# A lower rank for batch 0's evacuations in the planned opening of an attention and mixing kernel

## The chip, the core and the metric

The kernel runs on one core of a Trainium2 chip. The metric is the device time of one execution in microseconds, lower is better. The core has TensorE (PE in the rows; its weight loads are PEld), VectorE (DVE), ScalarE (ACT), GpSimd (POOL) and SyncE (SP), on whose queue the kernel starts its transfers.

## The reference

There are 8 batches, 8 heads, 576 positions and head size 64. Heads 0 to 3 attend to a window of 32 positions, heads 4 to 7 to every fourth position of the last 128. The attention output, as `x` with 512 channels, is then mixed:

```
scores = where(mask, q @ k.T / 8, -1e9);  attn = softmax(scores);  x = attn @ v
theta = x @ w_theta                              # 512 x 512
zr, zi = x * cos(theta), x * sin(theta)
y = w_tok_r @ zr + w_tok_i @ zi                  # over the 576 positions
u = x + y
out = u + max(u @ w_ch, 0)
```

## The kernel before

Heads go in four pairs per batch; a pair (b, pr) has 9 blocks of 128 x 64 scores in two groups of 5 and 4 blocks (`g0` 0 and 5), each in one of two banks `s`. Its steps are: mask and scores on PE (L424, L468); maxima on DVE (`row_max`: L430, then a scaling, L438); exponentials on ACT (L485 from PSUM, L504 from SBUF), which release the score bank; one over the sum on DVE (L507, L508); the product on POOL (L510); the turn, eight 32x288 transposes on DVE, planned as four steps of two (L525), which releases the pair's buffer `P`, one of two; and `pv` on PE (L617). A pair's scores need a free `P` buffer. In batch 1, pairs 2 and 3, and in batch 2, pairs 0 and 1, the mask is a matmul of its own ahead of the scores (`mask_on_pe`).

The mixing of a batch has 16 units: 8 tokens (`token`, 27 matmuls of 128x288 in nine triples, L850) and 8 channel units (`chan`, 12 matmuls, L882). For batch 0 they take one of two banks `m`. When a token is done, `residual` evacuates it: a sum on DVE (L825), which releases the bank, a rounding copy on ACT (L828) and the rest on POOL (L830). When a channel unit is done, `finish` evacuates it on DVE (L859). All arithmetic with large weights is split into a rounded part and a rest, so the weights are unpacked and split in the opening: a load into a staging tile, DVE L332, ACT L334 and L340, DVE L342, ACT L350, POOL L352. The staging tiles are shared: the late token weights (half g=1, n = 0 to 4; tiles `late_wt_a`, `late_wt_b`) use u3, xh1, xh2, xh3, xh0, and the channel weights c = 0 to 3 (`late_wc`, staged in `st_wch`) use xh2, xh3, xh2, xh3 after them. So channel weight c = 0 is loaded when the late token weight n = 2 has been split, and c = 1 after n = 3.

The opening (all of batch 0, the pairs of batch 1, the first two pairs of batch 2 and the thetas of batch 1) is ordered when the program is built, by the class `Order`. Each step is a generator that gives an engine and an estimated duration, or an event to wait for. Per engine, whoever is ready when the engine comes free and has the lowest rank goes next; a step's successor is ready only a latency after it (100 ns on PE and DVE, 130 on ACT and POOL, 1,800 for a load):

```
at = starts[eng]
t = min((t for t in ready if t[4] == eng and t[2] <= at), key=lambda t: (t[0], t[1]))
end = at + t[5]
self.free[eng] = end
self.now = end + LATENCY[eng]
```

The order that comes out is fixed: on the chip every engine runs its list from first to last. Ranks that matter: channel weights 2.1 to 2.13, token and channel units 2.95, evacuations 4.49 (RANK["evacuate"], used by `residual` and `finish` alone), scores and turns of batch 1's pairs 0 to 3 4.02, 4.23, 4.44 and 4.65, late token weights 6.75 to 6.79, scores and turns of batch 2's pairs 7.3 and 7.51, `pv` and what follows it 8.0 and up. The loads stand in one list too (SP). The later batches are laid down in loops, without ranks.

Of the kernel before, what the change touches and what calls it, by code (L numbers as in the profile page):

```python
# [30 lines left out]
LATE = ("u3", "xh1", "xh2", "xh3", "xh0")  # L31
LATE2 = ("xh2", "xh3", "xh2", "xh3")
RANK = dict(load=6.64, scores0=1.09, flip=0.01, pv0=1.13, pair=.21, theta_unpack=1.54, theta0=5.3, trig0=2.41,
            token_early=2.55, theta_split=6.42, token_late=6.75, chan=2.1, units=2.95, evacuate=4.49,
            scores1=4.02, scores2=7.3, pv1=8.0, theta1=5.96, trig1=7.42)
STS = (4, 0, 1, 2, 3)

# [1021 lines left out]
```

## Time and profile before

| | |
|---|---|
| time, median of 3 runs (lowest to highest) | 577.86 us (577.52 to 578.83) |
| the profiled execution: its time, its span | 577.82 us, 576.0 us |
| busy: PE, DVE, ACT, POOL | 550.5 us (96%), 378.0 (66%), 345.2 (60%), 222.2 (39%) |
| mean granted TensorE clock | 0.988 |

The span runs from the first to the last instruction. A granted clock of 1.00 is the full rate of 2.4 GHz, 0.50 is 1.2 GHz. Idle time of an engine other than the one that sets the end costs nothing by itself.

### The profile page before, as it was taken

What the parts mean: (1) busy time and instruction counts of PE and PEld (TensorE: products, weight loads), DVE (VectorE), ACT (ScalarE), POOL (GpSimd) and SP (SyncE); (2) the same over time, 40 slices, a digit from 0 to 9 for tenths busy, and PEclk for the clock granted to TensorE, in tenths of its full rate; (3) what the DMA queues carried; (4) which work ended last, traced back from release to release, by engine and by line L of the source; (5) the groups of instructions that cost most, each with busy time, mean ns of one, the idle gap of its engine ahead of it and who ended that gap; (6) DMA issues with size and microseconds to landing.
All of it is one profiled execution on the core that took longest, in us unless ns stands there. A gap on an engine that the chain in (4) does not pass through costs nothing.

```text
span 576.0 us, 13996 instructions
## 1 busy us (share of the span) xinstructions
PE 550.5 (96%) x5464; PEld 501.6 (87%) x5464; DVE 378.0 (66%) x1156; ACT 345.2 (60%) x939; POOL 222.2 (39%) x206
## 2 busy tenths in 40 slices
PE   5997799999999999999999999999999999999997
PEld 4744688879999899988999899988999899989997
DVE  3879798865666668756776768756775767445112
ACT  1498967768555784369555785359556695266110
POOL 2228855525224352226324253226323353325220
PEclk9999699899999999999999999999999999999999
DMA  8991437601747046540746146550747123321002
GB/s 303 400 368 28 165 105 245 216 0 63 231 150 193 32 162 210 169 127 20 268 143 172 64 148 202 181 136 11 252 146 190 69 83 102 77 89 65 18 1 83
DMA packets 45586, 81.91 MB, mean 142 GB/s; under 512 B 3920, under 2 KB 19024, under 8 KB 45520
## 3 DMA queue, kind: packets, MB, share of 16 engines
q1 hardware_dynamic: 45520, 81.02, 43.7%
q8 instruction: 43, 0.70, 0.5%
q14 instruction: 23, 0.19, 0.1%
HBM read 64.49 MB, written 16.52 MB: 141 GB/s over the span
## 4 chain that ended last, share of the span: by engine, by line
DVE 34%; ACT 30%; PE 25%; issue 5%; POOL 2%; DMA 2%; SPq 0%; ACTq 0%; POOLq 0%; DVEq 0%
DVE pt L525 16%; PE y L850 11%; ACT P L504 11%; PE c L882 6%; PE th L685 3%; DVE P L409 3%; ACT K L698 3%; ACT K L787 3%; DVE xh L599 3%; ACT th L796 2%; ACT zh L644 2%; DVE xq L729 2%; DVE K L789 2%; ACT cos L705 2%; ACT x L581 2%
## 5 line engine op out<-in xcount | busy, mean ns | idle before, releaser
L830 POOL TENSOR_TENSOR u<-x,u 128x288 fp32r<-128x288 f32 x64 | 54.7, 858 | 184.6 <-ACT u L828 184.6
L525 DVE STREAM_TRANSPOSE pt<-P 32x288 f32<-32x288 f32 x224 | 105.1, 469 | 12.0 <-POOL P L510 8.9
L882 PE MATMUL c<-u,late_wc 128*128 128x288 f32 x768 | 110.2, 296 | 2.8 <-DVE x L859 2.8
L882 PEld LDWEIGHTS c<-u,late_wc 128*128 128x128 f32 x768 | 106.0, 188 | 6.8 <-DVE x L859 4.0
L850 PE MATMUL y<-wtkh,zh 128*128 128x288 f32 x288 | 90.3, 314 | 1.1 <-ACT zh L644 1.1
L850 PE MATMUL y<-wtkh,zl 128*128 128x288 f32 x288 | 86.2, 299 | 4.0 <-POOL zl L646 4.0
L646 POOL TENSOR_TENSOR zl<-g,zh 128x512 fp32r<-128x512 f32 x40 | 52.3, 1316 | 97.5 <-ACT zh L644 84.5
L504 ACT ACTIVATE P<-P,mx 128x64 f32<-128x64 f32 x216 | 72.0, 335 | 25.8 <-DVE mx L498 25.8
L850 PE MATMUL y<-wtkl,zh 128*128 128x288 f32 x288 | 85.9, 298 | 0.0
L828 ACT CAST u<-x 128x288 fp32r<-128x288 f32 x64 | 26.9, 429 | 86.2 <-DVE x L825 85.5
L685 PE MATMUL th<-wthh,xh 128*128 128x512 f32 x224 | 74.8, 395 | 0.3 <-DVE g L784 0.3
L850 PE MATMUL y<-late_wt_b,zh 128*128 128x288 f32 x320 | 68.1, 297 | 0.0
L825 DVE TENSOR_TENSOR x<-y,x 128x288 f32<-128x288 f32 x64 | 28.1, 448 | 53.6 <-PE y L850 53.5
L850 PEld LDWEIGHTS y<-wtkh,zl 128*128 128x128 f32 x288 | 55.1, 191 | 4.7 <-POOL zl L646 4.7
L850 PEld LDWEIGHTS y<-wtkh,zh 128*128 128x128 f32 x288 | 54.9, 191 | 4.7 <-ACT zh L644 2.3
L850 PE MATMUL y<-late_wt_a,zh 128*128 128x288 f32 x256 | 56.3, 301 | 0.0
L850 PEld LDWEIGHTS y<-wtkl,zh 128*128 128x128 f32 x288 | 55.1, 191 | 0.3 <-issue 0.3
L510 POOL TENSOR_TENSOR P<-P,sm 128x576 f32<-128x576 f32 x32 | 37.5, 1172 | 41.1 <-DVE sm L508 18.1
L850 PEld LDWEIGHTS y<-late_wt_b,zh 128*128 128x128 f32 x320 | 51.4, 189 | 0.3
L685 PEld LDWEIGHTS th<-wthh,xh 128*128 128x128 f32 x224 | 42.0, 188 | 9.2 <-DVE g L784 0.6
L850 PE MATMUL y<-late_wt_b,zl 128*128 128x288 f32 x160 | 47.4, 296 | 0.0
L581 ACT COPY x<-o 128x576 f32<-128x576 f32 x32 | 29.4, 919 | 28.4 <-PE o L617 19.1
(108 smaller groups left out, 1106.3 us busy)
## 6 DMA issues: line engine op xcount, KB each, us to landing
q<-in_qT_dram SPq DMA_DIRECT2D x32, 576.0 KB, 5.2
va<-in_vw_dram SPq DMA_DIRECT2D x30, 320.0 KB, 3.2
k<-in_kT_dram SPq DMA_DIRECT2D x28, 304.0 KB, 5.5
out_dram<-x SPq DMA_DIRECT2D x28, 288.0 KB, 2.4
vb<-in_vw_dram SPq DMA_DIRECT2D x29, 256.0 KB, 3.8
xd<-xq SPq DMA_DIRECT2D x24, 288.0 KB, 5.1
xn<-xd SPq DMA_DIRECT2D x24, 256.0 KB, 3.4
st_wtk<-in_wtk_dram SPq DMA_DIRECT2D x8, 576.0 KB, 8.8
```

The costliest lines, as they stand in the source:

```text
L409: pin(nc.vector.tensor_tensor_reduce(out=P[:, n], in0=ps[:, n - g0], in1=mskb[:, mask_of(pr, n)], op0=ALU.add, op1=ALU.max, scale=1.0, sca ...
L504: table(nc.scalar.activation(P[:, n], P[:, n], AF.Exp, bias=mx[:, n:n + 1], scale=SCALE, accum_out=sm[:, n:n + 1]))
L510: pin(nc.gpsimd.tensor_tensor(P, P, sm.unsqueeze(2).to_broadcast([128, NJ, BW]), op=ALU.mult))
L525: pin(nc.vector.transpose(pmats[b, pr][k0:k0 + QB, :, hh, QB * e:QB * e + QB], P[p0:p0 + QB, :, QB * o:QB * o + QB]))
L581: pin(nc.scalar.copy(dst, src))
L646: pin(nc.gpsimd.tensor_tensor(lo, z, hi.bitcast(F32), op=ALU.subtract))
L685: pe(nc.tensor.matmul(pt, l, r, start=(n == 0), stop=(n == 3 * NC - 1)))
L825: pin(nc.vector.tensor_tensor(x[:, ts], ps, x[:, ts], op=ALU.add))
L828: pin(nc.scalar.copy(uh[b, d][:, ts], x[:, ts]))
L830: pin(nc.gpsimd.tensor_tensor(ul[b, d][:, ts], x[:, ts], uh[b, d][:, ts].bitcast(F32), op=ALU.subtract))
L850: pe(nc.tensor.matmul(ps, l[:, cs], r, start=(n == 0), stop=(n == 3 * NK - 1)))
L882: pe(nc.tensor.matmul(ps, l[:, cs], r[:, ts], start=(n == 0), stop=(n == 3 * NC - 1)))
```

## The change

One number of the table of ranks: the evacuations of batch 0 get 3.79 in place of 4.49. The work is the same. Where an evacuation and a step of rank 4.02, 4.23 or 4.44 (scores, exponentials and turns of batch 1's pairs 0 to 2) are ready on one engine, the evacuation now goes first. All that is planned after the first such place can move.

```
-            token_early=2.55, theta_split=6.42, token_late=6.75, chan=2.1, units=2.95, evacuate=4.49,
+            token_early=2.55, theta_split=6.42, token_late=6.75, chan=2.1, units=2.95, evacuate=3.79,
```

## Rows read from the trace of the kernel before

**Rows 1.** Busy time by stretch of the span; the first line names the columns.
```profile
core 0: us, PE busy (x) PEld busy (x) DVE busy (x) ACT busy (x) POOL busy (x), PEclk, DMA share, GB/s
82.47:101.51 19.04, 17.09 (x231) 15.35 (x231) 16.57 (x37) 15.17 (x53) 11.39 (x10) 1.00 0.69 238
101.51:106.50 4.99, 4.99 (x52) 4.23 (x51) 3.40 (x11) 2.87 (x12) 1.47 (x2) 0.66 0.82 273
106.50:143.00 36.50, 35.15 (x249) 31.61 (x247) 25.72 (x49) 27.37 (x58) 17.78 (x16) 1.00 0.17 60
143.00:576.00 433.00, 426.91 (x4177) 403.07 (x4176) 269.55 (x907) 245.03 (x693) 152.11 (x146) 1.00 0.42 127
```

**Rows 2.** Waits of PE, whole span: line, releaser: total us, times, longest.
```profile
PE s L424 <- ACT P L485: 3.0, 2, 2.0
...
PE c L882 <- DVE x L859: 2.8, 5, 0.6
```

**Rows 3.** Timeline of PE: start, us, line, operation, [idle before it and releaser].
```profile
72.79 0.29 PE L850 MATMUL y<-wtkh,zl 128*128 128x288 f32 x1
...
77.73 0.29 PE L850 MATMUL y<-wtkh,zl 128*128 128x288 f32 x1
...
82.47 0.31 PE L424 MATMUL s<-mskb,idb 128*128 128x64 bf16 x5 [1.04 <-ACT P L485]
...
101.51 0.30 PE L424 MATMUL s<-mskb,idb 128*128 128x64 bf16 x2 [1.95 <-ACT P L485]
...
120.27 0.49 PE L685 MATMUL th<-wthh,xh 128*128 128x512 f32 x1 [0.33 <-DVE g L784]
...
125.11 0.63 PE L759 MATMUL xn<-idt,x 128*128 128x128 f32 x4 [1.02 <-DVE g L750]
```

**Rows 4.** Timeline of DVE, 72 to 99 us.
```profile
72.40 1.25 DVE L342 SCALAR_TENSOR_TENSOR st_wtk<-st_wtk 128x576 uint32<-128x576 uint32 x1
73.67 3.85 DVE L525 STREAM_TRANSPOSE pt<-P 32x288 f32<-32x288 f32 x8
77.56 0.46 DVE L825 TENSOR_TENSOR x<-y,x 128x288 f32<-128x288 f32 x1
...
79.02 0.49 DVE L430 TENSOR_REDUCE mx<-s 128x5 f32<-128x320 f32 x1
79.55 0.96 DVE L525 STREAM_TRANSPOSE pt<-P 32x288 f32<-32x288 f32 x2
80.54 0.17 DVE L438 TENSOR_SCALAR mx<-mx 128x5 f32<-128x5 f32 x1
...
81.39 1.79 DVE L342 SCALAR_TENSOR_TENSOR st_wtk<-st_wtk 128x576 uint32<-128x576 uint32 x3
...
84.77 1.30 DVE L438 TENSOR_SCALAR mx<-mx 128x5 f32<-128x5 f32 x1
...
98.17 0.49 DVE L430 TENSOR_REDUCE mx<-s 128x5 f32<-128x320 f32 x1
```

**Rows 5.** Timeline of ACT: first and last exponential of batch 2's first group.
```profile
99.88 0.31 ACT L485 ACTIVATE P<-s,mx 128x64 f32<-128x64 f32 x1 [0.93 <-DVE mx L438]
...
101.05 0.32 ACT L485 ACTIVATE P<-s,mx 128x64 f32<-128x64 f32 x1
```

**Rows 6.** Timeline of POOL, 71 to 88 us.
```profile
71.88 1.15 POOL L510 TENSOR_TENSOR P<-P,sm 128x576 f32<-128x576 f32 x1
...
84.60 1.45 POOL L352 TENSOR_TENSOR late_wt_b<-st_wtk,late_wt_b 128x576 fp32r<-128x576 f32 x1 [0.76 <-ACT late_wt_b L350]
86.00 1.15 POOL L510 TENSOR_TENSOR P<-P,sm 128x576 f32<-128x576 f32 x1
```

**Rows 7.** Instructions of tile st_wch: ns min/median/max, first and last start.
```profile
L325 SPq DMA_DIRECT2D st_wch<-in_wch_dram x4: 327/328/423, 86.2 to 99.6; - x4
L332 DVE TENSOR_SCALAR st_wch<-st_wch x4: 424/428/1005, 91.1 to 105.4; 128x512 f32<-128x512 f32 x4
...
DMA to landing us min/median/max: 3.6/4.7/5.6
```

## The prediction

> **What bounds the kernel now.** I read first the busy shares by stretch [rows 1]. From 143 us to the end PE is busy 426.91 of 433.00 us at full clock; what is lost there is outside the planned part. PE has a fixed list of work, so the change can gain only by taking away PE's waits in the opening, or a stretch at half clock, and can lose only by bringing some. Next the waits of PE [rows 2]: in the planned part behind the first evacuation, two for exponentials on ACT (L485) make 3.0 us. PE's timeline places them [rows 3]: 1.04 us at 82.47 (pair 3 of batch 1) and 1.95 us at 101.51 (pair 1 of batch 2), and later 0.33 and 1.02 us in the thetas. Behind the second one the granted clock is 0.66 over 4.99 us [rows 1], a mix of full rate and half rate; behind the first it stays 1.00. At half rate that stretch lost 4.99 x (1 - 0.66) = 1.70 us. No wait of PE names an evacuation of batch 0's tokens: the one for L859, 2.8 us, stands in channel units behind 143 us (five waits of at most 0.6 us). So the moved instruction itself is not what PE waits for; the result hangs on how the rest of the list falls.
>
> Then DVE, which feeds both waits [rows 4, 5]. The second wait's bank is released by exponentials at 99.88 to 101.05, these follow maxima at 98.17 on DVE, and DVE was busy 16.57 of 19.04 us from 82.47 to 101.51 [rows 1]: the maxima stood in a queue.
>
> **Step 1, the move itself.** Token 1 ends at 72.79 + 0.29 = 73.1 us [rows 3]; its sum on DVE runs at 77.56, behind eight transposes (73.67, 3.85 us) [rows 4]. These are turn steps of pairs 0 and 1, ranks 4.02 and 4.23, all below 4.49 and above 3.79. With 3.79 the sum goes after the first two, at about 74.6. It costs 0.46 us in both places, and its bank is not needed before token 2 ends (77.73 + 0.29 = 78.0 [rows 3]), where it was just free anyway: gain for PE, nothing. The first evacuation already goes as soon as its token is done, the third falls into the 100 ns in which a competitor isn't ready, the others compete on either side with ranks that stay on their side (4.65, 7.3, 7.51). The copies on ACT and POOL that follow are the same instructions; the exponentials behind which they might push in wait for later maxima, so I cost them at nothing; if one does stand in front, it is a copy's length, under half of the sum of 0.46 that went before it on DVE.
>
> **Step 2, what falls differently behind it.** Two turns alternate on DVE, since a turn's next step is ready 100 ns after its last. The evacuation now takes the slot in between, so pair 0's last step is ready when it ends and goes ahead of pair 1's first. Pair 0's buffer is released one step (0.96 us [rows 4]) sooner in the list, and the scores of pair 2 come two token triples earlier on PE. Then follows a slot in which pair 1 is in its 100 ns and only late weights are ready: L342 of n = 2, the first of the three at 81.39 (1.79 / 3 = 0.60 us each [rows 4]), moves there, to about 77. The scaling L438 (80.54) that starts the first wait's exponentials then has one turn step less (0.96) and one L342 more (0.60) ahead: 0.36 earlier. PE reaches its mask one triple earlier too, with the triple done behind it. Cost on PE's first wait: 0, between -0.4 and +0.4.
>
> **Step 3, the weights.** On POOL the split of n = 2 stands at 84.60 (1.45 us) in front of pair 2's product at 86.00 [rows 6]. Moved some five us ahead, it frees the product to run 1.4 us sooner, and the turn of pair 2 behind it. It also releases the staging tile of channel weight 0, whose load is issued at 86.2 and first unpacked at 91.1 [rows 7]: about 80 and 85. Each weight's unpack is one L332 (0.43 [rows 7]) and one L342 (0.60 [rows 4]) on DVE, about 1.0 us, which leaves the full stretch before 98.17. Pair 2's buffer comes free earlier, so the scores of batch 2's pair 0 come two or three triples earlier on PE, and their maxima wait in a shorter queue. Sum for the maxima at 98.17: 1.4 (turn) + 1.0 (weight 0) and about as much as the scores move, 1.2: 3.6 us earlier. The mask at 101.51, by contrast, keeps its place in PE's list: the plan ties it to pair 3's turn. It needs the exponentials 1.95 us earlier than they come; 3.6 covers it. If only the turn's 1.4 comes, 0.55 stays.
>
> What could be late next is what stands behind the channel weight's load: DVE's L332 in front of pair 3's maxima, ACT's L334 in front of pair 3's exponentials. The plan gives a load 1.46 us of transfer and 1.8 of latency, 3.3; the rows say 3.6 to 5.6, median 4.7 [rows 7]. DVE then stands 0.3 to 2.3 us. What hides it: the next mask that needs these banks (batch 2, pair 0) stands some six triples later, and a triple is between 0.31 us (3 x 426.91 / 4177, the mean matmul behind 143 us [rows 1]) and 0.87 us (3 x 0.29, one record alone [rows 3]); since records overlap I take 0.4, so 2.4 us. Without that cover it is PE that waits.
>
> **Sum.** -1.95 (wait at 101.51) - 1.70 (half rate behind it) + 0 (first wait) + 0.65 (about half of the two waits of 0.33 and 1.02 that the thetas show now [rows 3], for small new ones) = -3.0 us. The profiled execution took 577.82 us, 1.8 of it around its span of 576.0, and the median of the runs is 577.86, so the two agree; 577.82 - 3.0 = 574.8.
>
> **A rule against it.** L342 at 72.40 took 1.25 us and ended at 73.65, 0.62 after POOL's product (71.88, 1.15) [rows 4, 6]; three in a row at 81.39 took 1.79, 0.60 each. L438 at 84.77 took 1.30, to the end of the split at 84.60 + 1.45 [rows 4, 6]. So DVE stands behind POOL at times, by up to 1.1 us. The Trainium skill, SBUF — State Buffer, section "SBUF: two separate sides", says that the pair of ports that VectorE and GpSimd share is an exclusive lock, and that whoever comes second waits for the whole instruction. The trace agrees (1.25 against 0.60). By that rule a product moved onto L332 and L438 holds pair 3's maxima by up to 1.15 us; since the split that held L438 at 84.77 goes away, the sum by the rule is the same -3.0 or, if the hold comes on top, -1.9.
>
> **Rivals.**
> 1. *The queue only changes shape.* DVE's work is the same, and 87% busy; the exponentials of batch 2 come out as late relative to PE's list as now, because the plan's durations are short of the chip's (a turn step 0.96 against 0.94 planned, a maximum 0.49 against 0.40), and a wait of about 2 us turns up at this mask or the next. For it: the order is made so that PE takes whatever is just ready, so new tight places appear where old ones go. Against: the weights really leave that stretch. Time 577.82 - 0.6 to + 0.6 (about half of the smaller wait, 1.04, either way), a little below the middle since the weights do move: 577.6.
> 2. *The load blocks (slower).* The channel weight's load lands later than the cover of 2.4 us behind its planned time; DVE and ACT, which run their lists in order, hold pair 3's maxima and exponentials, PE waits for pair 3's banks, and the mask at 101.51 stays late. Deciding point: a landing over 5.6 us, or an issue that comes late behind the queue of loads of q and k. Price: a new wait of 1.0 to 1.95 us, with half rate behind it as at 101.51 up to 1.70: 578.8 to 581.5, say 579.5. For it: DVE's wait for such a load is already seen, L332 of 1,005 ns at most and landings up to 5.6 [rows 7]. The Trainium skill, TensorE: Matmul & The Clock Gate, section "Architectural detail: the array is 16× 32×32, not 1× 128×128", has ScalarE and VectorE as strict first-in first-out; by that rule nothing passes a load that is late, and the time is rival 2's if the load is late enough, else the forecast's.
> 3. *Both waits go.* The exponentials at 82.47 also come in time: a further -1.04 and the thetas' 0.65 not paid: 573.1.
>
> **How the numbers follow.** The forecast has 0.48, rival 1 0.24, rival 2 0.20, rival 3 0.08. The forecast's own range is 573.8 (no new small waits, and 0.4 off the first) to 576.4 (the lock's 1.1 and 0.5 left of the wait). A change below 0.2% (1.16 us) can't be told from none here. Rival 1 is mostly within it, with a little of it on either side; the forecast is nearly all below 576.7. So faster 0.58, same 0.22, slower 0.20. For 8 in 10 the range goes from rival 3, 573.1, to the lower half of rival 2, 579.0.
>
> **What the profile would show.** Right: the second L825 of batch 0 in front of the third transpose pair of its run; an L342 of the late weights among the transposes, some 4 us sooner; the product of pair 2 right behind its sum, with the split gone from in front; the first `st_wch` load some 6 us sooner; the maxima of batch 2's first group 3 to 4 us sooner; no wait of PE over 1 us at the mask of batch 2's pair 1 and the granted clock 1.00 from 82 to 143 us. Wrong would be a wait of PE for L485 at another mask, DVE idle in front of L332 for a load, with ACT behind it, or a stretch at half clock at another place.

## The result, and the profile after

The change made the kernel slower by a little: median 579.34 us (576.68 to 582.40, 22 runs) against 578.03 us (575.68 to 579.68, 22 runs) before, a ratio of 1.003 with a 95% interval of 1.0017 to 1.0042. The forecast was 574.8 us.

The profiled execution of the changed kernel took 582.4 us (span 580.6), the longest of its 22, so its 4.6 us over the profile of before are not all the change's. To compare like with like I count from the first evacuation of batch 0 (the first L825: at 68.46 before, at 70.20 after); up to there both kernels have the same lists. From it to the first L859 behind 500 us, deep in the part that the change doesn't reach, before needs 440.73 us and after 443.58. The other 1.7 us are older than the change's first place. So is a little of the 2.85: over the first 6.54 us from that evacuation the granted clock was 0.72 after and 0.79 before, some 0.4 us, and it was back at 1.00 before the first moved instruction ran (75.97).

Busy time by stretch after; the first line names the columns, and the second stretch is the 9 us from the second mask on:

```profile
core 0: us, PE busy (x) PEld busy (x) DVE busy (x) ACT busy (x) POOL busy (x), PEclk, DMA share, GB/s
83.63:102.97 19.34, 16.26 (x225) 14.54 (x225) 18.56 (x38) 14.79 (x52) 10.85 (x9) 1.00 0.69 239
102.97:111.97 9.00, 8.51 (x94) 7.34 (x93) 8.20 (x22) 8.04 (x34) 4.10 (x4) 0.62 0.72 253
70.20:513.78 443.58, 435.65 (x4406) 406.86 (x4406) 308.94 (x992) 278.36 (x807) 173.79 (x162) 0.99 0.44 137
```

The last two of these before:

```profile
101.51:110.51 9.00, 9.00 (x107) 8.00 (x107) 7.16 (x19) 6.88 (x28) 3.21 (x3) 0.81 0.78 258
68.46:509.19 440.73, 433.60 (x4405) 405.04 (x4404) 306.96 (x992) 278.35 (x809) 173.23 (x162) 0.99 0.45 138
```

PE's idle time in it (the length less its busy time) grew from 7.13 to 7.93 us, and its busy time by 2.05 us with one matmul more on record: the same matmuls at half clock for longer. Most of that stands behind the second mask. In the 9 us from it the granted clock was 0.62 after and 0.81 before, so half clock lost 9.00 x (1 - 0.62) = 3.4 us in place of 1.7. DVE between the two masks went from 16.57 of 19.04 us [rows 1] to 18.56 of 19.34: it has become fuller, not emptier.

Waits of PE at the masks, from its timeline after:

```profile
83.63 0.31 PE L424 MATMUL s<-mskb,idb 128*128 128x64 bf16 x5 [0.25 <-ACT P L485]
102.97 0.30 PE L424 MATMUL s<-mskb,idb 128*128 128x64 bf16 x2 [3.08 <-ACT P L485]
105.77 0.37 PE L424 MATMUL s<-mskb,idb 128*128 128x256 bf16 x1 [0.48 <-ACT P L485]
```

Of the two waits of [rows 3], the first fell from 1.04 to 0.25 us; the second, which was to go, grew from 1.95 to 3.08, and its second group adds 0.48. The half clock behind it did not go: it lasted about twice as long.

The mask also stands at another place in PE's list. The matmuls of L850 from 60 us up to it (PE busy, PEld busy, clock, DMA share, GB/s), first before, then after:

```profile
60.00:101.50 41.50, 26.92 (x153) 23.06 (x153) 0.91 0.49 168
60.00:102.96 42.96, 25.97 (x144) 22.23 (x144) 0.88 0.50 170
```

That is nine matmuls, three token triples, fewer ahead of it; at full clock three triples take about 1.2 us (those just ahead of the wait start 0.40 us apart).

DVE's timeline after, the instructions that answer to [rows 4] and those that now stand among them:

```profile
75.97 0.46 DVE L825 TENSOR_TENSOR x<-y,x 128x288 f32<-128x288 f32 x1
76.46 1.94 DVE L525 STREAM_TRANSPOSE pt<-P 32x288 f32<-32x288 f32 x4
78.43 0.76 DVE L342 SCALAR_TENSOR_TENSOR st_wtk<-st_wtk 128x576 uint32<-128x576 uint32 x1
...
86.47 1.40 DVE L332 TENSOR_SCALAR st_wch<-st_wch 128x512 f32<-128x512 f32 x1 [0.21 <-DMA st_wch<-in_wch_dram]
87.79 1.42 DVE L438 TENSOR_SCALAR mx<-mx 128x5 f32<-128x5 f32 x1
...
95.82 1.38 DVE L332 TENSOR_SCALAR st_wch<-st_wch 128x512 f32<-128x512 f32 x1
...
98.09 0.49 DVE L430 TENSOR_REDUCE mx<-s 128x5 f32<-128x320 f32 x1
98.51 0.69 DVE L342 SCALAR_TENSOR_TENSOR st_wch<-st_wch 128x512 uint32<-128x512 uint32 x1
99.12 0.45 DVE L825 TENSOR_TENSOR x<-y,x 128x288 f32<-128x288 f32 x1
99.61 0.95 DVE L525 STREAM_TRANSPOSE pt<-P 32x288 f32<-32x288 f32 x2
100.59 0.71 DVE L438 TENSOR_SCALAR mx<-mx 128x5 f32<-128x5 f32 x1
```

Before, what followed the maximum of 98.17 was this, on DVE:

```profile
98.17 0.49 DVE L430 TENSOR_REDUCE mx<-s 128x5 f32<-128x320 f32 x1
98.69 0.95 DVE L525 STREAM_TRANSPOSE pt<-P 32x288 f32<-32x288 f32 x2
99.67 0.17 DVE L438 TENSOR_SCALAR mx<-mx 128x5 f32<-128x5 f32 x1
```

POOL after, the tile of the channel weights, and ACT at the exponentials:

```profile
80.03 1.44 POOL L352 TENSOR_TENSOR late_wt_b<-st_wtk,late_wt_b 128x576 fp32r<-128x576 f32 x1 [1.57 <-ACT late_wt_b L350]
...
86.43 1.15 POOL L510 TENSOR_TENSOR P<-P,sm 128x576 f32<-128x576 f32 x1 [1.22 <-ACT late_wt_b L350]
87.54 2.41 POOL L352 TENSOR_TENSOR late_wt_b<-st_wtk,late_wt_b 128x576 fp32r<-128x576 f32 x2
...
95.30 1.61 POOL L510 TENSOR_TENSOR P<-P,sm 128x576 f32<-128x576 f32 x1 [0.85 <-DVE sm L508]
...
99.98 1.29 POOL L352 TENSOR_TENSOR late_wc<-st_wch,late_wc 128x512 fp32r<-128x512 f32 x1 [1.61 <-ACT late_wc L350]
```

```profile
L325 SPq DMA_DIRECT2D st_wch<-in_wch_dram x4: 328/328/600, 81.5 to 101.3; - x4
L332 DVE TENSOR_SCALAR st_wch<-st_wch x4: 429/905/1398, 86.5 to 105.6; 128x512 f32<-128x512 f32 x4
...
DMA to landing us min/median/max: 3.9/4.5/5.8
```

```profile
99.24 0.67 ACT L350 CAST late_wc<-st_wch 128x512 fp32r<-128x512 f32 x1 [0.76 <-DVE st_wch L342]
...
100.13 1.19 ACT L581 COPY x<-o 128x576 f32<-128x576 f32 x1
101.34 0.31 ACT L485 ACTIVATE P<-s,mx 128x64 f32<-128x64 f32 x1
```

Read together, in time from the first evacuation: the maximum L430 of batch 2's first group came at 27.89 us in place of 29.71, 1.82 earlier. Behind it L342 of channel weight 1 and token 4's sum now stand, beside the transpose pair that stood there before, ahead of the scaling L438, which itself lasts 0.71 in place of 0.17: its end is at 31.10 against 31.38 before. ACT's copy L581, which runs behind weight 1's L350 and so behind the same L342, ends at the same point (101.32), so both hold the first exponential: 31.14 against 31.42 before, 0.28 us earlier. PE, however, stood at the mask at 29.69 (102.97 - 3.08 - 70.20) against 31.10 before, 1.41 us earlier: it had waited 0.8 us less on the way and had three triples fewer to do, less some 0.6 us by which it was behind from the start (two matmuls, and half clock for longer). It arrived sooner at a bank that was released when it always was: 1.95 - 0.28 + 1.41 = 3.08.

Three instructions on DVE in this stretch lie beside POOL's and are long. L332 at 86.47 started 0.04 behind POOL's product (86.43, 1.15) and lasted 1.40 in place of 0.43; the 128x5 scaling at 87.79 started inside a split and lasted 1.42 in place of 0.17; L332 at 95.82 started inside the next product and lasted 1.38. The five instructions concerned (L438 of pair 3's two groups and of batch 2's first, L332 of weights 0 and 1) took 1.30, 0.75, 0.17, 0.43 and 1.00 us before, 1.42, 0.17, 0.71, 1.40 and 1.38 after: 1.4 us more, and so most of the 2 us by which DVE is fuller.

### The profile page after: what moved, and what is told of

It is laid out like the page before. It is cut to its first block, busy times and chain, and to the rows that moved or that the text cites. A ratio compares the mean times of both kernels' runs of the same rounds, so it can differ in the third digit from the quotient of the medians.

```text
span 580.6 us, 13998 instructions
## 1 busy us (share of the span) xinstructions
PE 552.8 (95%) x5464; PEld 503.8 (87%) x5464; DVE 380.0 (65%) x1156; ACT 345.5 (60%) x939; POOL 222.9 (38%) x206
## 4 chain that ended last, share of the span: by engine, by line
DVE 34%; ACT 29%; PE 27%; issue 4%; DMA 3%; POOL 2%; SPq 0%; ACTq 0%; DVEq 0%; POOLq 0%
DVE pt L525 16%; PE y L850 12%; ACT P L504 10%; PE c L882 6%; PE th L685 3%; DVE P L409 3%; ACT K L698 3%; ACT K L787 3%; DVE xh L599 2%; ACT th L796 2%; ACT zh L644 2%; DVE K L789 2%; DVE xq L729 2%; ACT cos L705 2%; POOL P L510 2%
## 5 line engine op out<-in xcount | busy, mean ns | idle before, releaser
L850 PE MATMUL y<-wtkh,zh 128*128 128x288 f32 x288 | 90.3, 313 | 1.9 <-ACT zh L644 1.9
L850 PE MATMUL y<-wtkh,zl 128*128 128x288 f32 x288 | 86.5, 300 | 4.0 <-POOL zl L646 4.0
L850 PE MATMUL y<-wtkl,zh 128*128 128x288 f32 x288 | 86.1, 299 | 0.0
L850 PE MATMUL y<-late_wt_b,zh 128*128 128x288 f32 x320 | 68.8, 299 | 0.0
L825 DVE TENSOR_TENSOR x<-y,x 128x288 f32<-128x288 f32 x64 | 28.2, 450 | 55.3 <-PE y L850 55.2
L850 PEld LDWEIGHTS y<-wtkh,zh 128*128 128x128 f32 x288 | 55.3, 192 | 5.3 <-ACT zh L644 3.0
L850 PEld LDWEIGHTS y<-wtkh,zl 128*128 128x128 f32 x288 | 55.2, 192 | 4.8 <-POOL zl L646 4.8
L850 PE MATMUL y<-late_wt_a,zh 128*128 128x288 f32 x256 | 56.5, 302 | 0.0
L850 PEld LDWEIGHTS y<-wtkl,zh 128*128 128x128 f32 x288 | 55.4, 192 | 0.3 <-issue 0.3
L850 PEld LDWEIGHTS y<-late_wt_b,zh 128*128 128x128 f32 x320 | 51.7, 190 | 0.3
L850 PE MATMUL y<-late_wt_b,zl 128*128 128x288 f32 x160 | 47.7, 298 | 0.0
L581 ACT COPY x<-o 128x576 f32<-128x576 f32 x32 | 29.2, 913 | 28.2 <-PE o L617 23.5
```

What stands on the lines that cost most here:

```text
L581: pin(nc.scalar.copy(dst, src))
L825: pin(nc.vector.tensor_tensor(x[:, ts], ps, x[:, ts], op=ALU.add))
L850: pe(nc.tensor.matmul(ps, l[:, cs], r, start=(n == 0), stop=(n == 3 * NK - 1)))
```

## The experiments

The first column is the ratio to the kernel before, with its 95% interval. The last two are read from one profile each, over the same work as above (first L825 to the first L859 behind 500 us): PE's idle time, and its busy time, which grows with half clock (about 432 without). For the two with fillers the busy time holds these too. After and only_t1 have the same lists, and their two profiles differ by 1.05 us of idle and 2.70 of busy time: smaller differences in these two columns say nothing about a kernel.

| kernel | ratio | median (runs) | idle | busy |
|---|---|---|---|---|
| before | 1 | | 7.13 | 433.60 |
| after | 1.0030 [1.0017, 1.0042] | 579.34 (22) | 7.93 | 435.65 |
| only_t1 | 1.0014 [0.9996, 1.0033] | 578.23 (12) | 8.98 | 432.95 |
| not_t1 | 1.0034 [1.0015, 1.0052] | 579.41 (12) | 9.42 | 432.53 |
| after_fill | 1.0023 [1.0004, 1.0043] | 579.08 (12) | 6.46 | 436.18 |
| before_fill | 1.0002 [0.9986, 1.0018] | 577.81 (12) | 6.12 | 435.15 |
| after_later | 1.0045 [1.0025, 1.0064] | 580.88 (12) | 10.75 | 431.92 |
| before_later | 1.0053 [1.0035, 1.0071] | 581.22 (6) | 9.09 | 433.69 |
| after_act | 0.9999 [0.9983, 1.0016] | 577.62 (12) | 6.91 | 433.06 |
| before_act | 0.9990 [0.9974, 1.0007] | 577.09 (12) | 7.21 | 432.47 |
| after_s2 | 1.0022 [1.0008, 1.0036] | 579.41 (12) | 8.84 | 432.33 |
| before_s2 | 1.0051 [1.0032, 1.0069] | 581.21 (6) | 8.67 | 435.34 |
| after_s2_act | 1.0000 [0.9985, 1.0015] | 578.20 (12) | 8.02 | 433.13 |
| before_s2_act | 1.0002 [0.9985, 1.0018] | 578.69 (12) | 7.94 | 434.54 |
| after_chan | 1.0048 [1.0029, 1.0066] | 580.56 (12) | 8.33 | 433.85 |
| before_chan | 1.0078 [1.0059, 1.0097] | 582.14 (6) | 10.78 | 433.65 |

**Which evacuation.** only_t1 is the kernel before with the new rank for token 1's evacuation alone; not_t1 is the changed kernel without it.

```
-        go(residual(b, d, g, ps, rel), RANK["evacuate"])
+        go(residual(b, d, g, ps, rel), 3.79 if (b, d, g) == (0, 1, 0) else RANK["evacuate"])
```

> Kernel before, with rank 3.79 for the evacuation of token 1 alone (token d=1 of the first half). Its lists on every engine come out the same as those of the changed kernel. If the move of step 1 is the whole change: PE waits about 3.1 us for L485 at the mask of batch 2's pair 1 and about 0.25 us at that of pair 3, and the time is 1.002 to 1.005 of before. If the profile of the changed kernel was slow by chance (4.6 us of span, where the medians differ by 1.3): the waits are the same, the span is nearer 577 to 579, and the stretches at half clock differ in place or length from those of the first profile.

> Changed kernel, with rank 4.49 kept for the evacuation of token 1 and 3.79 for all the others. The prediction says that the others keep their places: then the waits are those of before (1.04 and 1.95 us, half clock behind the second) and the ratio is 0.998 to 1.002. The rival: the others move work too, later (their lists do differ from before's from token 3 on), and then the second wait differs by more than 0.5 us and the ratio can be off 1 by 0.003 either way.

The lists of only_t1 are those of the changed kernel, instruction by instruction on every engine. Its ratio, 1.0014, and the change's, 1.0030, are thus two measurements of one program, and their intervals overlap; only_t1 alone, with 12 runs, would not be told from no change. Its profile shows the same exponentials (98.92, which is 31.15 behind the first evacuation, against 31.14) and another split of the waits. PE's timeline of only_t1, then ACT's and DVE's:

```profile
95.88 0.69 PE L617 MATMUL o<-pt,vb 128*64 128x64 f32 x16 [1.43 <-DMA vb<-in_vw_dram]
100.56 0.30 PE L424 MATMUL s<-mskb,idb 128*128 128x64 bf16 x2 [1.41 <-ACT P L485]
103.36 0.27 PE L424 MATMUL s<-mskb,idb 128*128 128x256 bf16 x1 [0.78 <-ACT P L485]
```

```profile
98.92 0.31 ACT L485 ACTIVATE P<-s,mx 128x64 f32<-128x64 f32 x1
```

```profile
84.39 1.05 DVE L332 TENSOR_SCALAR st_wch<-st_wch 128x512 f32<-128x512 f32 x1 [0.56 <-DMA st_wch<-in_wch_dram]
...
94.36 0.43 DVE L332 TENSOR_SCALAR st_wch<-st_wch 128x512 f32<-128x512 f32 x1 [0.89 <-DMA st_wch<-in_wch_dram]
```

Here a load of v landed late and took 1.43 us of what the mask took in the other execution. DVE's two L332 were held less, and DVE stood for their loads instead; the exponentials came at the same point. not_t1 departs from the order of the kernel before at token 2's sum and costs 1.0034: the claim that the other evacuations stay where they were holds only when token 1's has moved; left alone, they move too, and lose as much. Its wait at the second mask is gone; 1.14 us for a load of v and up to 1.85 in the thetas stand in its place.

**Half clock.** 18 matmuls of 128x384 into a spare bank ahead of the mask of batch 2's pair 1 (12 in before_fill), so that PE has work while it waits:

```
+                if (b, pr, g0) == (2, 1, 0):
+                    for _ in range(18):
+                        pe(nc.tensor.matmul(pf[:, :6 * BW], idb, mskb.rearrange("p a b -> p (a b)"),
+                                            start=True, stop=True))
```

> Changed kernel, with 18 extra matmuls (128x384, no use made of them) on PE in front of the mask that waits, about 3 us at full clock. They fall into the wait. If the half clock behind a wait is a loss of its own beside the wait: no stretch at half clock from 82 to 143 us, and 1 to 2.5 us less than the changed kernel in the median (ratio 0.998 to 1.000), with fewer of its runs over 580 us. If the half clock costs little, or the extra work delays the mask as much as it saves: ratio 1.002 to 1.006.

> Kernel before, with 12 such matmuls (about 2 us) at the same mask. If the half clock is a loss of its own: no half clock from 82 to 143 us, ratio 0.997 to 0.999. If it is not: 1.000 to 1.003.

The granted clock is 1.00 from 82 to 143 us in both profiles. after_fill still takes 1.0023, and before_fill 1.0002: half clock in this place is not a loss of its own that can simply be taken away. PE's timeline shows one reason, first in the changed kernel, then in after_fill and before_fill (whose line numbers are 7 higher):

```profile
123.21 0.51 PE L685 MATMUL th<-wthh,xh 128*128 128x512 f32 x1 [0.36 <-DVE g L784]
```

```profile
121.19 0.50 PE L692 MATMUL th<-wthh,xh 128*128 128x512 f32 x1 [0.99 <-DVE g L791]
```

```profile
122.10 0.50 PE L692 MATMUL th<-wthh,xh 128*128 128x512 f32 x1 [1.22 <-DVE g L791]
```

PE comes to the thetas sooner (51.01 us behind the first evacuation in place of 52.65, and 51.11 in place of 51.48) and waits there longer for DVE: 0.99 and 1.22 us in place of 0.36 and 0.33 [rows 3]. Part of what half clock took comes back as waiting.

**The wait itself.** The scores of batch 2's pair 1 wait, in the plan, for the end of a token, so that PE does that work first:

```
+        if (b, pr) == (2, 1):
+            yield None, ("tk", 0, 2, 1)
```

> Changed kernel, with the scores of batch 2's pair 1 put behind token 6 in the plan, so that PE has eight triples (about 3.2 us at full clock) to do before the mask that waited 3.08 us. If that wait is PE's own loss: it goes (under 0.5 us), with the half clock behind it, PE's idle time from the first evacuation on falls by 2.5 to 3.5 us, and the time to 0.994 to 0.997 of before. If DVE's and ACT's queue sets the end of the opening (shape theory): the idle time comes back at the thetas (waits for DVE L784 and L750 grow from 0.36 and 0.99 by about what the mask saves), ratio 0.999 to 1.004.

> Kernel before, with the same delay of batch 2's pair 1. If the wait of 1.95 us is PE's own loss: it goes with the half clock behind it, ratio 0.993 to 0.997. If DVE's queue sets the end: the waits of the thetas (0.33 and 1.02 us) grow by about as much, ratio 0.998 to 1.003.

The wait at the mask is gone in both, and both ratios lie above all that was expected. before_later is slower than the kernel that it comes from, and after_later, at 1.0045, isn't told from the change's 1.0030. PE's timeline of after_later, whose line numbers are 2 higher from the edit on:

```profile
106.51 0.69 PE L619 MATMUL o<-pt,vb 128*64 128x64 f32 x16 [2.62 <-DMA vb<-in_vw_dram]
120.14 0.66 PE L884 MATMUL c<-u,late_wc 128*128 128x288 f32 x3 [2.37 <-DVE x L827]
```

and of before_later:

```profile
114.44 4.43 PE L884 MATMUL c<-u,late_wc 128*128 128x288 f32 x21 [3.71 <-DVE x L827]
```

PE did the tokens early and met, some 10 us on, the same engines late: DVE hadn't evacuated them (2.37 and 3.71). The 2.62 us of after_later are for a load of v.

**The scaling off DVE.** The 128x5 and 128x4 scalings of the maxima go to ACT; no other list changes.

```
-            pin(nc.vector.tensor_scalar(mx[:, g0:g1], mx[:, g0:g1], -SCALE, None, op0=ALU.mult))
+            pin(nc.scalar.activation(mx[:, g0:g1], mx[:, g0:g1], AF.Copy, scale=-SCALE))
```

> Changed kernel, with the scaling of the maxima (L438, pairs whose mask is a matmul) done on ACT in front of its exponentials in place of DVE; all lists else the same. Holds theory (DVE instructions stand behind POOL's and that makes batch 2's exponentials late): the two held scalings (1.42 and 0.71 us against 0.17) leave DVE, the wait at the mask of batch 2's pair 1 falls from 3.08 to between 1.0 and 1.9 us, and the time to 0.998 to 1.001 of before. Shape theory (DVE's and ACT's queue is as long as ever and PE only comes to it sooner): the wait stays within 0.4 of 3.1 us and the ratio at 1.002 to 1.004.

> Kernel before, with the same scaling on ACT. Holds theory: the scaling held at 84.77 (1.30 us) and the one at 99.67 behind two transposes leave DVE; the second wait falls from 1.95 to under 1.2 us, the half clock behind it may go, ratio 0.994 to 0.998. Shape theory: the wait stays within 0.4 of 1.95 us, ratio 0.999 to 1.001.

after_act takes 0.9999, without the change's cost; its interval ends just below that of the change, but overlaps that of only_t1, which has the change's lists. Its exponentials of batch 2's first group start at 98.75, 29.22 us behind the first evacuation (69.53; 31.14 in the changed kernel). ACT, PE and DVE of after_act:

```profile
97.67 0.21 ACT L438 ACTIVATE mx<-mx 128x5 f32<-128x5 f32 x1
97.78 1.20 ACT L581 COPY x<-o 128x576 f32<-128x576 f32 x1
98.75 0.30 ACT L485 ACTIVATE P<-s,mx 128x64 f32<-128x64 f32 x1
```

```profile
100.37 0.30 PE L424 MATMUL s<-mskb,idb 128*128 128x64 bf16 x2 [1.27 <-ACT P L485]
```

```profile
86.29 0.64 DVE L332 TENSOR_SCALAR st_wch<-st_wch 128x512 f32<-128x512 f32 x1 [0.96 <-DMA st_wch<-in_wch_dram]
...
95.60 0.49 DVE L430 TENSOR_REDUCE mx<-s 128x5 f32<-128x320 f32 x1
```

Taking the small scaling out of DVE's queue brings the exponentials 1.9 us forward and PE's wait from 3.08 to 1.27, with no half clock from 82 to 143 us (only_t1's profile, too, has 1.41 and no half clock). Of the 1.9 us, 1.82 are there at the maximum (26.07 us behind the first evacuation in place of 27.89): they come from further up on DVE, where pair 3's scaling of 1.42 us is gone and L332 lasts 0.64 in place of 1.40, and not from the scaling behind this maximum. The edit removes the hold by POOL and the place in DVE's list at once; the run doesn't part the two. On the kernel before, whose scalings were held by 1.1 and 0.6 us, the same edit gives 0.9990, not told from none; the theory of the holds had expected 0.994 to 0.998.

**The maxima in front of everything.** Scores, maxima and exponentials of batch 2's pairs at rank 2.0, then the same with the scaling on ACT:

```
-        go(scores(2, p), RANK["scores2"] + p * RANK["pair"])
+        go(scores(2, p), 2.0 + p * .01)
```

> The changed kernel with scores, maxima and exponentials of batch 2's pairs at rank 2.0 and 2.01 in place of 7.3 and 7.51: the two scalings and the second maximum of batch 2's pair 0 (L438, L430, L438) now stand on DVE directly behind L342 of channel weight 1, ahead of token 4's sum and of the turn of batch 1's pair 3; the mask of batch 2's pair 1 goes one token triple later in PE's list. Theory A, the maxima stand behind other work in DVE's queue: the wait of 3.08 us for L485 at that mask falls under 1.0 us and no new one over 1.2 us comes in its place; ratio to before 0.996 to 0.999. Theory B, DVE's and ACT's work as a whole sets the opening, whatever goes first: the wait turns up elsewhere (for the turn of pair 3 at pv, for a channel weight, or in the thetas, 1 to 3 us); ratio 1.001 to 1.005.

> The kernel before with the same two ranks for batch 2's scores (2.0 and 2.01). Theory A: the wait of 1.95 us at the mask of batch 2's pair 1 falls under 0.8 us, and with it the half clock behind it; ratio to before 0.994 to 0.998. Theory B: the wait turns up elsewhere, ratio 0.999 to 1.004.

> The changed kernel with the ranks 2.0 and 2.01 for batch 2's scores and the scaling (L438) on ACT. Theory A: ratio 0.994 to 0.998. Theory B: as the changed kernel with the scaling on ACT alone, 1.000, within 0.998 to 1.002.

> The kernel before with both the ranks 2.0 and 2.01 for batch 2's scores and the scaling of the maxima (L438) as an activation on ACT, so that no scaling on DVE can be held by POOL. Theory A and the holds add up: ratio 0.993 to 0.998. Theory B: as before with the scaling on ACT alone, 0.999, within 0.997 to 1.001.

In after_s2 the exponentials start at 95.98, 28.06 us behind the first evacuation: 3.1 earlier than in the changed kernel, nearly what the forecast's step 3 wanted. PE doesn't wait at that mask any more. Its timeline shows the waits that came in its place:

```profile
104.13 0.69 PE L617 MATMUL o<-pt,vb 128*64 128x64 f32 x16 [1.35 <-DMA vb<-in_vw_dram]
...
116.58 1.06 PE L882 MATMUL c<-u,late_wc 128*128 128x288 f32 x6 [0.59 <-DVE x L825]
118.37 0.50 PE L685 MATMUL th<-wthh,xh 128*128 128x512 f32 x1 [0.73 <-DVE g L784]
123.21 0.63 PE L759 MATMUL xn<-idt,x 128*128 128x128 f32 x4 [1.01 <-DVE g L750]
```

With 0.33 and 0.67 us at 112 and 113 that is 4.7 us (the last two stood in the changed kernel as 0.36 and 0.99), and the time, 1.0022, is not told from that of the change. On the kernel before it is worse, 1.0051, above both expected ranges: PE waits 2.29 us for a channel weight's split and 1.50 for a sum, and the granted clock is 0.84 from 104 to 125 us, with half clock at another place than before. Theory A falls: with the wait taken away by the way that it should have gone, nothing was won. With the scaling on ACT both return to 1.000, the value of theory B; for the kernel before this is the clearest step of all the runs (1.0051 to 1.0002, intervals far apart).

**The channel weights.** Their unpacking at rank 4.7 in place of 2.1, so that it gives way to evacuations, scores and turns:

```
-            token_early=2.55, theta_split=6.42, token_late=6.75, chan=2.1, units=2.95, evacuate=3.79,
+            token_early=2.55, theta_split=6.42, token_late=6.75, chan=4.7, units=2.95, evacuate=3.79,
```

> The changed kernel with the channel weights' unpacking at rank 4.7 in place of 2.1: it gives way to evacuations, scores and turns of batch 1, weight 1's L342 stands behind the maxima and the turn of pair 3, and the load of weight 1 behind k of batch 2's pair 0. Theory A, the channel weights that the change brought forward stand in front of the exponentials and cost the 0.3%: the wait at the mask of batch 2's pair 1 falls under 1.5 us, ratio to before 0.998 to 1.000. Theory B, DVE's and ACT's work as a whole sets the opening: the wait comes back there or at another place (vb, a channel weight, the thetas), ratio 1.001 to 1.005.

> The kernel before with the channel weights' unpacking at rank 4.7 in place of 2.1. Theory A: the wait of 1.95 us at the mask of batch 2's pair 1 shrinks, since two unpackings no longer stand ahead of it, ratio 0.996 to 0.999. Theory B: a wait of the same size there or elsewhere, ratio 0.999 to 1.004.

before_chan lost 0.8%, twice what either theory allowed, and after_chan gained nothing: the weights that come early are not the cost. PE's timeline of after_chan shows the wait where it was:

```profile
103.25 0.43 PE L424 MATMUL s<-mskb,idb 128*128 128x64 bf16 x2 [3.35 <-ACT P L485]
```

## Why the prediction was wrong

**Right.** Steps 1 and 2 fell as written in the lists: token 1's sum ahead of three transpose pairs (75.97), L342 of late weight n = 2 among the transposes (78.43; 8.2 us behind the first evacuation, against 12.9 for the first of its three in [rows 4]), its split away from in front of pair 2's product (80.03 and 86.43), the first load of a channel weight at 81.5 in place of 86.2 and unpacked at 86.5 in place of 91.1 [rows 7]. The first wait fell by 0.79 in this profile, more than the 0.4 allowed, but that isn't the change's: in other profiles with the same lists up to there it was 0.25 to 1.28 us with the change (only_t1 0.48, after_s2 1.28) and 0.40 to 1.13 without (before_s2, before_chan). Rival 2 has the number, 579.5, but its mechanism isn't what the profile shows: one landing took 5.8 us, over its 5.6, but DVE waited 0.21 us in all for the channel weights' loads. It isn't excluded either: only_t1 shows waits of 0.56 and 0.89 in front of L332, the kernel before 0.51.

**The step that failed** is the sum in step 3, "3.6 us earlier", with the mask that "keeps its place in PE's list". The maximum gained 1.82 us, the exponentials that release the bank 0.28, since the scaling behind the maximum got a channel weight, a sum and a hold in front of it, and ACT's copy came behind the same channel weight. I moved the maximum and forgot that the scaling is a step of its own, which queues again. What moved away in one place (weight 0 and the split) came back in another (weight 1 and token 4). And the mask didn't keep its place: it stands three token triples earlier in PE's list, and PE stood there 1.41 us sooner. So -1.95 and -1.70 in the sum became, in this profile, +1.13 (3.08 in place of 1.95), +0.48 for the second group and +1.7 for half clock that lasted twice as long; with -0.79 at the first wait and the 0.4 that are older that is about the 2.85 us. The exponentials and the mask's place come back in only_t1; how the loss shows at PE, as a wait or as half clock, does not.

**The holds.** The rule against it was weighed and put at no more than 1.1 us, balanced by the split's going. The rows show three holds of 0.95 to 1.25 us and one of 0.54 between 86 and 102 us, 1.4 us more than before. By the rule of the Trainium skill, SBUF — State Buffer, section "SBUF: two separate sides", a VectorE instruction that needs the port pair shared with GpSimd and a GpSimd instruction exclude each other, and the one that starts first keeps the pair for its whole length. The trace agrees, for a product against L332 (1.40 to 0.43) and for a split against a 128x5 scaling (1.42 to 0.17), while a maximum (80.21) and transposes (80.73) beside POOL's split of 80.03 kept their 0.49 and 0.95. That these holds make the change's loss isn't shown. after_act, which takes the scalings out of them, comes back to 1.000, as after_s2_act does; but in only_t1 the L332s were held by 0.6 us in place of 1.9, DVE stood for their loads instead, and the exponentials came no sooner.

**The rival that came nearest** is the first: the queue only changes shape. Its price was set at ±0.6 us about nothing, from half of a wait; the medians gave +1.3. The experiments show its mechanism: six ways to remove or shift the wait at this mask (later, first, the channel weights back, each on both kernels) put waits at v's loads, at channel units for sums, at channel weights or in the thetas, or left one at this mask (3.35 and 3.79 us), and none beat the kernel that it came from by more than the measurement can tell. Only taking the scalings off DVE helped, clearly so from before_s2 to before_s2_act. What stays open is how the 1.3 us divide. Each timed run lists its span and mean granted clock; span times (1 - clock), an estimate of what half clock took, is on average 6.9 us over the changed kernel's 22 runs and 6.2 over 110 runs of the kernel before, and the rest of the span 570.9 against 569.8 (means; the medians differ by less). That would be 0.7 us of half clock and 1.1 of waits. But only_t1's 12 runs, the same lists, have 5.3 and 571.5; the 34 together have 6.4 and 571.1, so that a share of half clock isn't shown. after_fill's 12 runs have 5.0 and 572.5 (with the fillers): what half clock no longer took came back in the rest.

No version measured beats both kernels: before_act, at 0.9990, has an interval that reaches 1.0007.

## What to carry to other kernels

A gain that is forecast for one step of a chain must be followed through every step behind it that queues again on a full engine, down to the instruction that releases the buffer; here the maximum came 1.8 us sooner and the release 0.3. Where a wait is the visible end of an engine that is 87 to 96% busy over the stretch, as here, every reordering tried moved the wait or left it, and only taking work from that engine brought the time back. And look at when the waiting engine arrives: if the waiting step itself comes earlier in its engine's list, the wait grows by as much. Before a wait in one profile is explained, see whether a second execution of the same lists has it too.

## What the runs showed that I had not expected

A 128x5 scaling that takes 0.17 us lasted 1.42 behind POOL's split: the smaller the instruction on the chain, the more of its cost is where it starts. The same instruction lists gave 576.5 to 582.4 us (34 runs of the changed kernel and only_t1), while the kernel before stayed within 575.7 to 579.7 in its 22: a change of order can widen the spread as well as move the median. In one profile PE's loss stands as 3.08 us at one wait with half clock behind it, in another as 1.43 and 1.41 at two without. In after_chan and before_chan, too, half clock stood behind single waits of 3.35 and 3.79 us (granted clock 0.67 and 0.74 over the 5 us from 101.5).
